# A planned instruction order, searched anew: the chain of chunks gets a margin in its due times

## The chip, the cores and the metric

One Trainium2 chip, one of its cores. The time is the device time of one execution in microseconds (us); the number for a kernel is the median of several executions. TensorE (PE) does the matrix products, PEld is its loading of weights, VectorE (DVE), ScalarE (ACT) and GpSimd (POOL) work on elements, and SyncE (SP) issues most of the transfers from and to the chip's memory.

## What is computed

Two stages, one after the other. The first is a delta rule over a sequence: 32 independent heads (4 x 8), 768 steps, head width 48. The second is a feed-forward block on the 3,072 tokens that come out.

```python
for t in range(S):                      # 768 steps, for all B*H = 32 heads
    y[t] = q[t] @ state                 # state: 48 x 48 per head
    v_old = k_n[t] @ state              # k_n: keys, normalised
    state += beta[t] * outer(k_n[t], v[t] - v_old)
x = y.reshape(3072, 384)
h = x @ w_in                            # 384 x 2048
out = (h - tanh(h)) @ w_out             # 2048 x 384
```

## The kernel before, in words

The 768 steps are cut into 24 **chunks** of 32 steps. Inside a chunk the recurrence is solved as a triangular system, and from chunk to chunk only the state is carried. For each chunk `s` TensorE runs small stages of 32 matmuls on 32- or 48-wide pieces:

- `score(s)` (line 456): products of keys with keys and queries. Four chunks make a group `g`, and `solve(g)` inverts their triangular systems on DVE, about a hundred short dependent steps (lines 501 to 588, mostly 577 and 579) that end in the transposition `tt` (line 588).
- `chain()` runs the chunks in order: keys on the state (L672), queries on the state (L689), the solution applied (L704, needs `tt` of its group and the values after the subtraction on L679), the update of the state (L719, then two additions on L745), the rest of the result (L729), and in `output()` the transposition of the chunk's result (L764) into `xt`, the tokens of the second stage.

Four chunks make a **window** of 512 tokens. For each window the feed-forward block runs 16 times two **units** on TensorE: `hidden` (L875, 9 matmuls of 128x128 on 512 columns into `ph`) and `out_units` (L925, 9 more, summed up in `po`). Between them `gate` works on ACT and DVE: tanh (L892), the subtraction (L894, which frees `ph`), and a split of the result into two parts (L900, L902). The first `F0` pairs of window 0 run as two halves of 256 columns, so that they can begin before all four chunks are there. The weights are decoded at the start (`decode`, `piece`; L823, L832, L833). Where the planner sees nothing else for TensorE early on, `warm()` puts in a **filler**, one matmul of zeros on 512 columns (L356).

All instructions are emitted by a planner, the class `Plan`. Each piece of work is an `Op` with an engine, a cost in us, its dependencies and a due time. `Plan.run` takes the engine that can begin first; among its Ops that could begin within `SLACK[engine]` of the first one it chooses the smallest `value`: the start plus `URGENCY` times the due time, plus a random part (`WHIM`), plus `STICK` on TensorE where the kind of work changes. The chosen order is fixed for each engine: at run time an engine works in this order and waits at an instruction whose inputs are missing. The planner also keeps a model of TensorE's supply with instructions (`settle`, `fetched`, `span`): 512 at the start, then 256 at a time.

Due times come from a few numbers. `start(w)` is when window `w` should begin (`SECOND + PITCH*(w-1)`), `need(s)` when chunk `s` should be ready, `unit_due(w, f)` spreads the units over a window, and `QUIRK` shifts single generators by their name. `LATCH` holds a score back until an earlier chunk is solved. `loads()` issues transfers on SP as buffers come free: keys `kc` after a score, keys `kd` after L689, values `v` after L719. `refill()` issues the last weight loads on ACT (`AHEAD`, `BEHIND`).

The due times of the chunks are these two lines (306 to 309 hold them):

```python
start = lambda w: SECOND + PITCH * (w - 1) if w else OPEN
need = lambda s: start(s // W) - SPREAD * (W - 1 - s % W) if s >= W else FIRST_NEED + NEXT_NEED * s
```

Of the kernel before, what the change touches and what calls it, by code (L numbers as in the profile page):

```python
# [26 lines left out]
W = 4  # L27
# [58 lines left out]
class Plan:  # L86
    ENGINES = ("PE", "DVE", "ACT", "POOL", "SP")
    OVERLAP = {"PE": 0.0, "DVE": 0.085, "ACT": 0.085, "POOL": 0.0, "SP": 0.0}
    VISIBLE = {"PE": 0.13, "DVE": 0.06, "ACT": 0.06, "POOL": 0.06, "SP": 0.0}
    SLACK = {"PE": 0.264, "DVE": 14.746, "ACT": 0.22, "POOL": 0.2, "SP": 0.0}  # L90

    def __init__(self, tc, nc):
        self.tc, self.nc, self.dice = tc, nc, random.Random(SEED)
# [165 lines left out]
def kernel(ctx: ExitStack, tc: tile.TileContext, kq, vk, beta, w_in, w_out, const, out):  # L259
# [46 lines left out]

    ISSUE = 0.45
    start = lambda w: SECOND + PITCH * (w - 1) if w else OPEN
    need = lambda s: start(s // W) - SPREAD * (W - 1 - s % W) if s >= W else FIRST_NEED + NEXT_NEED * s
    solve_due = lambda g: need(4 * g) - 9.0 if g else 30.0  # L310

    def opening():
# [750 lines left out]
```

## Time and profile before

| | |
|---|---|
| median of 3 executions | 622.18 us (621.96 to 623.24) |
| the profiled execution, its own time | 623.54 us |
| its span, first to last instruction | 621.8 us |
| TensorE busy | 602.0 us, 97% of the span |
| VectorE, ScalarE, GpSimd busy | 378.5, 221.5, 46.3 us |
| mean granted TensorE clock | 0.988 of full speed |
| moved from and to memory | 51.54 MB, 83 GB/s on the mean |

The profile comes from one execution. Its page gives busy times, the wait chain that ended last and the costliest groups; the trace behind it can be asked for single instructions. A row of the timeline reads: start, duration, engine, line, operation, output<-inputs, shapes, count, and in brackets the idle time before it and what ended that. A float32 stage of 32 matmuls stands in the timeline as x64, since each goes through TensorE twice.

### The profile page before, as it was taken

How to read it: one execution, taken by the hardware profiler on the slowest of the kernel's cores; microseconds unless marked ns; L12 is line 12 of the kernel's file. 1: busy time of each engine (PE TensorE's matmuls, PEld its weight loads, DVE VectorE, ACT ScalarE, POOL GpSimd, SP SyncE). 2: the span in 40 equal slices, each digit the busy share in tenths (PEclk: the TensorE clock that was granted, in tenths of full speed). 3: DMA queues.
4: the chain of work that ended last, by engine and by line, in shares of the span. 5: the costliest groups of instructions: out<-in, count | busy, mean ns of one | idle time of the engine just before them, and what ended most of it. 6: DMA issues, size and time to landing. Idle time of an engine off the chain costs nothing.

```text
span 621.8 us, 24085 instructions
## 1 busy us (share of the span) xinstructions
PE 602.0 (97%) x11120; PEld 470.8 (76%) x11120; DVE 378.5 (61%) x827; ACT 221.5 (36%) x396; POOL 46.3 (7%) x60
## 2 busy tenths in 40 slices
PE   6999999989998999999989999999999999999996
PEld 4545778867786878788778888878788887878884
DVE  2998778863789458776254788237789323432332
ACT  1324645665322342323322232333234213332332
POOL 1211100001200021000011000001100000000000
PEclk9899999999999999999999999999999999999999
DMA  9991222253332131222330212021120100010001
GB/s 321 391 374 35 99 67 74 86 163 103 97 105 70 61 113 54 63 72 76 91 108 29 77 55 78 35 64 34 55 79 35 36 2 3 3 52 1 0 1 51
DMA packets 24500, 51.54 MB, mean 83 GB/s; under 512 B 2512, under 2 KB 2640, under 8 KB 24400
## 3 DMA queue, kind: packets, MB, share of 16 engines
q1 hardware_dynamic: 22912, 46.77, 22.6%
q10 hardware_dynamic: 1488, 3.24, 1.7%
q8 instruction: 87, 1.43, 0.9%
q14 instruction: 13, 0.11, 0.1%
HBM read 45.29 MB, written 4.72 MB: 80 GB/s over the span
## 4 chain that ended last, share of the span: by engine, by line
PE 94%; DVE 2%; issue 2%; ACT 1%; DMA 0%; ACTq 0%; DVEq 0%
PE ph L875 33%; PE po L925 32%; PE po L356 7%; PE psa L456 4%; PE psa L719 3%; PE psa L704 3%; PE psy L729 3%; PE psa L672 3%; PE psy L689 2%; PE ph L832 2%; PE psa L764 1%; DVE a L579 1%; DVE tmp L577 1%; PE ph L833 0%; DMA out<-o 0%
## 5 line engine op out<-in xcount | busy, mean ns | idle before, releaser
L875 PE MATMUL ph<-xt,w 128*128 128x512 f32 (+1 forms) x900 | 217.1, 390 | 5.3 <-issue 2.7
L925 PE MATMUL po<-gh,w 128*128 128x512 f32 (+1 forms) x900 | 218.2, 390 | 1.5 <-issue 1.2
L875 PEld LDWEIGHTS ph<-xt,w 128*128 128x128 f32 x900 | 163.3, 190 | 40.6 <-issue 2.9
L925 PEld LDWEIGHTS po<-gh,w 128*128 128x128 f32 x900 | 162.1, 189 | 36.5 <-issue 1.7
L894 DVE TENSOR_TENSOR t<-ph,t 128x512 f32<-128x512 f32 (+1 forms) x100 | 66.6, 668 | 95.7 <-ACT t L892 95.5
L892 ACT ACTIVATE t<-ph 128x512 f32<-128x512 f32 (+1 forms) x100 | 58.0, 580 | 185.8 <-PE ph L875 184.8
L902 DVE TENSOR_TENSOR gh<-t,gh 128x512 fp32r<-128x512 f32 (+1 forms) x100 | 67.8, 678 | 45.3 <-ACT gh L900 44.8
L900 ACT CAST gh<-t 128x512 fp32r<-128x512 f32 (+1 forms) x100 | 60.4, 604 | 70.7 <-DVE t L894 53.1
L579 DVE TENSOR_TENSOR a<-a,tmp 128x30 f32<-128x30 f32 (+9 forms) x180 | 61.0, 339 | 4.7
L577 DVE TENSOR_TENSOR tmp<-a 128x30 f32<-128x30 f32 (+9 forms) x180 | 60.3, 335 | 4.8
L356 PE MATMUL po<-wz 128*128 128x512 bf16 x176 | 44.8, 407 | 1.1 <-DVE idle L315 1.1
L745 DVE TENSOR_TENSOR st<-st,psa 112x384 f32<-112x384 f32 x44 | 22.6, 551 | 36.2 <-PE psa L719 35.7
L356 PEld LDWEIGHTS <-wz 128*128 128x128 bf16 x176 | 17.2, 103 | 23.6 <-issue 6.2
L478 POOL TENSOR_TENSOR pq<-pq,cs 128x256 f32<-128x256 f32 x24 | 19.0, 790 | 200.0 <-ACT pq L472 200.0
L650 POOL TENSOR_TENSOR v<-v,nt 128x384 f32<-128x384 f32 x20 | 18.2, 918 | 138.2 <-DMA v<-in_vk 69.7
L456 PEld LDWEIGHTS psa<-kc 48*32 48x32 f32 x1344 | 20.4, 110 | 7.1 <-issue 6.5
L719 PEld LDWEIGHTS psa<-u_sb,v 32*48 32x48 f32 x1472 | 18.8, 120 | 9.2 <-issue 7.9
L456 PE MATMUL psa<-kc 48*32 48x64 f32 x1344 | 23.9, 222 | 0.0
L754 ACT COPY y_sb<-psy 128x384 f32<-128x384 f32 x24 | 11.5, 479 | 34.3 <-PE psy L729 34.3
L770 DVE TENSOR_TENSOR xt<-psa,xt 128x384 fp32r<-128x384 f32 x24 | 13.3, 555 | 16.1 <-ACT xt L768 16.1
L704 PEld LDWEIGHTS psa<-v,tt 32*32 32x32 f32 x1536 | 17.9, 105 | 6.3 <-issue 2.8
L719 PE MATMUL psa<-u_sb,v 32*48 32x48 f32 x1472 | 21.7, 205 | 1.0 <-issue 1.0
(61 smaller groups left out, 415.2 us busy)
## 6 DMA issues: line engine op xcount, KB each, us to landing
kd<-in_kq SPq DMA_DIRECT2D x23, 512.0 KB, 4.0
kc<-in_kq SPq DMA_DIRECT2D x21, 512.0 KB, 3.8
v<-in_vk SPq DMA_DIRECT2D x24, 384.0 KB, 3.5
raw<-in_w_in SPq DMA_DIRECT2D x6, 768.0 KB, 11.8
raw<-in_w_out SPq DMA_DIRECT2D x6, 768.0 KB, 12.1
out<-o SPq DMA_DIRECT2D x18, 256.0 KB, 2.0
raw<-in_w_in ACTq DMA_DIRECT2D x2, 768.0 KB, 4.5
raw<-in_w_out ACTq DMA_DIRECT2D x2, 768.0 KB, 4.5
```

The costliest lines, as they stand in the source:

```text
L356: nc.tensor.matmul((ps if own else pos[w][0][0]).rearrange("p (a b) -> p a b", a=4), wz, wide, start=own, stop=own, skip_group_check=not own)
L456: nc.tensor.matmul(ps[quad[b], h, :], k[:, 0], k, start=True, stop=True)
L577: nc.vector.tensor_tensor(tv, col.broadcast_to(shape), row.broadcast_to(shape), ALU.mult)
L579: nc.vector.tensor_tensor(below, below, tv, ALU.add)
L704: nc.tensor.matmul(pu[rows, h, :], tt[rows, 8 * r + h, :], v[rows, h, :], start=True, stop=True)
L719: nc.tensor.matmul(hv(sums[b // 2][0])[HALF[b % 2], h, :], kt[rows, h, :], u_sb[rows, h, :], start=True, stop=True)
L875: nc.tensor.matmul(p, wi[f][:, a, ct, :], xt[:, b, ct, part], start=(ct == 0 and i == 0), stop=(ct == NC - 1 and i == 2))
L892: nc.scalar.activation(t_, p, AF.Tanh)
L894: nc.vector.tensor_tensor(t_, p, t_, ALU.subtract)
L900: nc.scalar.copy(gh[:, 0, :n], t_)
L902: nc.vector.tensor_tensor(gh[:, 1, :n], t_, gh[:, 0, :n].bitcast(F32), ALU.subtract)
L925: nc.tensor.matmul(po[c][:, part], wo[f][:, a, 128 * c:128 * c + 128], gh[:, b, :n], start=(f == 0 and i == 0 and z < 1), stop=(ended.get( ...
```

## The change

The program is the same; only the planner's numbers and one due time differ. `need(s)` loses a new constant `MARGIN` (7.6 us) for the chunks of window 1 and later. At the same time `SECOND`, `PITCH`, `SPREAD`, `LEAD`, `SLACK`, `STICK`, `HOLD`, `GUARD`, `FIRST_NEED`, `NEXT_NEED`, `EAGER`, `LATCH` and many `QUIRK` entries change, the random part goes (`WHIM` 0.5 to 0.0), `F0` rises from 4 to 6, the first loads stand in another order, and two weight loads move from SP to ACT (`AHEAD` 12 to 10).

```diff
-    SLACK = {"PE": 0.264, "DVE": 14.746, "ACT": 0.22, "POOL": 0.2, "SP": 0.0}
+    SLACK = {"PE": 0.211, "DVE": 14.4, "ACT": 0.344, "POOL": 0.2, "SP": 0.0}
...
-    need = lambda s: start(s // W) - SPREAD * (W - 1 - s % W) if s >= W else FIRST_NEED + NEXT_NEED * s
+    need = lambda s: start(s // W) - MARGIN - SPREAD * (W - 1 - s % W) if s >= W else FIRST_NEED + NEXT_NEED * s
...
-BURN, LATCH = 0, ((8, 0), (8, 5), (13, 5))
+BURN, LATCH = 0, ((9, 4), (10, 2), (16, 2))
...
-OPEN, SECOND, EARLY, PITCH, SPREAD, URGENCY, FETCH, QUEUED, FILL, LEAD, STICK = 60.5, 164.6, 4.4, 83.3, 19.1, 0.049, 3.5, 3.3, 150.0, 37.4, 0.1
-WARM, HOLD, GUARD, F0 = 120.0, 150.0, 0.28, 4
+OPEN, SECOND, EARLY, PITCH, SPREAD, URGENCY, FETCH, QUEUED, FILL, LEAD, STICK = 61.2, 176.5, 5.4, 87.8, 15.5, 0.049, 3.5, 3.3, 150.0, 29.7, 0.2
+WARM, HOLD, GUARD, F0 = 120.0, 90.0, 0.3, 6
...
-WHIM, SEED = 0.5, 240318
-FIRST_NEED, NEXT_NEED, EAGER, JOIN = 69.6, -6.7, 88.6, -61.2
-LOW, SPARE = True, 8
-AHEAD, BEHIND = 12, 3
+WHIM, SEED = 0.0, 495840
+FIRST_NEED, NEXT_NEED, EAGER, JOIN = 67.7, -1.8, -27.1, -62.0
+LOW, SPARE, MARGIN = True, 8, 7.6
+AHEAD, BEHIND = 10, 4
```

What the planner makes of it moves on every engine. Three places follow; in them the numbers behind names are buffers, `kd5` and `kc8` belong to chunks 5 and 8, `tt2` to group 2.

TensorE at chunk 5, before: the rows from the keys on the state to the next scores.

```order
L672 MATMUL psa1_88<-st_83,kd5_1224 32x48 x32
L689 MATMUL psy_2227<-st_83,kd5_1224 32x48 x32
L704 MATMUL psa0_87<-v_1126,tt1_1896 32x48 x32
L875 MATMUL ph_2303<-xt0_1030,w8_1804 128x512 x9
L875 MATMUL ph_2315<-xt0_1030,w10_2003 128x512 x9
L456 MATMUL psa1_88<-kc8_486 32x64 x32
L925 MATMUL po0_1300<-gh_2330,w9_1895 128x512 x3
L925 MATMUL po1_1301<-gh_2330,w9_1895 128x512 x3
L925 MATMUL po2_1302<-gh_2330,w9_1895 128x512 x3
L456 MATMUL psa0_87<-kc9_533 32x64 x32
```

The same place with the change:

```order
L672 MATMUL psa1_88<-st_83,kd5_1344 32x48 x32
L689 MATMUL psy_2274<-st_83,kd5_1344 32x48 x32
L925 MATMUL po0_1225<-gh_2236,w9_2079 128x512 x3
L925 MATMUL po1_1226<-gh_2236,w9_2079 128x512 x3
L925 MATMUL po2_1227<-gh_2236,w9_2079 128x512 x3
L875 MATMUL ph_2326<-xt0_942,w10_1881 128x512 x9
L704 MATMUL psa0_87<-v_1114,tt1_2041 32x48 x32
L456 MATMUL psa1_88<-kc8_493 32x64 x32
L875 MATMUL ph_2416<-xt0_942,w10_1881 128x512 x9
```

Before, three small stages (L672, L689, L704) stood in a row and two units behind them; now two units stand between the second and the third stage.

TensorE at the end of the program, window 5, before:

```order
L875 MATMUL ph_8830<-xt5_7737,w14_2263 128x512 x9
L925 MATMUL po0_8528<-gh_8828,w13_2139 128x512 x3
L925 MATMUL po1_8529<-gh_8828,w13_2139 128x512 x3
L925 MATMUL po2_8530<-gh_8828,w13_2139 128x512 x3
L875 MATMUL ph_8855<-xt5_7737,w14_2263 128x512 x9
L925 MATMUL po0_8528<-gh_8853,w15_2369 128x512 x3
L925 MATMUL po1_8529<-gh_8853,w15_2369 128x512 x3
L925 MATMUL po2_8530<-gh_8853,w15_2369 128x512 x3
L925 MATMUL po0_8528<-gh_8878,w15_2369 128x512 x3
L925 MATMUL po1_8529<-gh_8878,w15_2369 128x512 x3
L925 MATMUL po2_8530<-gh_8878,w15_2369 128x512 x3
```

And with the change:

```order
L875 MATMUL ph_8855<-xt5_7808,w12_2145 128x512 x9
L875 MATMUL ph_8865<-xt5_7808,w14_2341 128x512 x9
L875 MATMUL ph_8880<-xt5_7808,w14_2341 128x512 x9
L925 MATMUL po0_8582<-gh_8878,w13_2234 128x512 x3
L925 MATMUL po1_8583<-gh_8878,w13_2234 128x512 x3
L925 MATMUL po2_8584<-gh_8878,w13_2234 128x512 x3
L925 MATMUL po0_8582<-gh_8894,w15_2434 128x512 x3
L925 MATMUL po1_8583<-gh_8894,w15_2434 128x512 x3
L925 MATMUL po2_8584<-gh_8894,w15_2434 128x512 x3
L925 MATMUL po0_8582<-gh_8918,w15_2434 128x512 x3
L925 MATMUL po1_8583<-gh_8918,w15_2434 128x512 x3
L925 MATMUL po2_8584<-gh_8918,w15_2434 128x512 x3
```

Units of L875 and L925 took turns, and the last two L925 units followed the last L875 unit; now three of each stand together, and three L925 units follow the last L875 unit.

VectorE where the solution of group 2 (`tt2`) is finished, before:

```order
L577 TENSOR_TENSOR tmp_3355<-a2_2548 128x30
L579 TENSOR_TENSOR a2_2548<-a2_2548,tmp_3355 128x30
L894 TENSOR_TENSOR t_3317<-ph_3285,t_3317 128x512
L582 TENSOR_TENSOR a2_2548<-a2_2548,gm_2554 128x1024
L902 TENSOR_TENSOR gh_3360<-t_3317,gh_3360 128x512
L588 STREAM_TRANSPOSE tt2_3375<-a2_2548 128x32x32
L894 TENSOR_TENSOR t_3372<-ph_3345,t_3372 128x512
L894 TENSOR_TENSOR t_3386<-ph_3362,t_3386 128x512
L902 TENSOR_TENSOR gh_3390<-t_3372,gh_3390 128x512
L902 TENSOR_TENSOR gh_3424<-t_3386,gh_3424 128x512
```

With the change:

```order
L894 TENSOR_TENSOR t_3374<-ph_3343,t_3374 128x512
L577 TENSOR_TENSOR tmp_3475<-a2_2818 128x30
L579 TENSOR_TENSOR a2_2818<-a2_2818,tmp_3475 128x30
L582 TENSOR_TENSOR a2_2818<-a2_2818,gm_2824 128x1024
L902 TENSOR_TENSOR gh_3478<-t_3374,gh_3478 128x512
L679 TENSOR_TENSOR v_2217<-v_2217,psa0_87 128x384
L588 STREAM_TRANSPOSE tt2_3510<-a2_2818 128x32x32
L894 TENSOR_TENSOR t_3392<-ph_3364,t_3392 128x512
L894 TENSOR_TENSOR t_3508<-ph_3482,t_3508 128x512
L902 TENSOR_TENSOR gh_3578<-t_3392,gh_3578 128x512
```

The subtraction for chunk 8 (L679) now stands just ahead of `tt2`, and two subtractions of the gate (L894) still stand behind it.

Over the whole program, the counts that differ are these: fillers 176 before and 166 now; matmuls of L875 and of L925 on 512 columns 828 each before and 810 now, on 256 columns 72 each before and 108 now (and the gate's work on ACT and DVE with them). When the result of the fourth chunk of windows 1 to 5 is transposed (L764), TensorE has run 32, 64, 96, 127 and 160 units before the change, and 32, 63, 96, 128 and 159 with it (two halves counted as one unit).

More of the change, by code (lines that the diff above doesn't have):

```diff
@@ L996 @@
     return plan
-QUIRK = {'hidden0.1.2': 33, 'add7': 12, 'score5': -17, 'score6': -29, 'decode8': 35, 'vsub6': 18, 'out_units0.1.3': 40, 'piece13': -25, 'prep0': 3, 'mask3': -34, 'output3': -1, 'join0': 33, 'output4': -18, 'hidden0.-1.0': 12, 'output0': 14, 'chain7': 12, 'out_units0.0.1': 25, 'vsub3': -38, 'join6': 0, 'decode7': 14, 'prep6': 25, 'decode9': -40, 'piece8': 2, 'hidden0.-1.2': 10, 'vsub0': -18, 'hidden0.-1.3': 10, 'add0': 15, 'piece15': 40, 'prep7': -15, 'solve0': 8, 'decode14': -30, 'solve1': 5, 'gate0.-1.1': 2, 'mask1': -3, 'mask7': -22, 'join1': -2, 'mask6': 0, 'join2': -5, 'decode4': -26, 'out_units0.-1.0': 30, 'piece4': 2, 'out_units0.0.2': 22, 'score1': 3, 'hidden0.1.3': -15, 'decode6': 3, 'gate0.1.3': 7, 'chain0': -4, 'join3': 7, 'vsub1': 25, 'decode1': 24, 'out_units0.-1.3': 30, 'piece6': -10, 'gate0.-1.0': -22, 'hidden0.-1.1': 0, 'output7': 35, 'out_units0.-1.1': -5, 'gate0.1.2': -6, 'gate0.1.1': 2, 'decode2': -8, 'decode15': -3, 'vsub5': 20, 'score2': -5, 'score7': -34, 'decode11': 0, 'mask2': 0, 'score4': 0, 'piece11': 10, 'hidden0.0.3': -3, 'piece9': 10, 'triangle0': -10, 'decode5': 20, 'gate0.1.0': -25, 'piece1': -5, 'decode10': 40, 'chain2': 3, 'gate0.0.2': 18, 'join7': -20, 'vsub7': 4, 'chain5': -6, 'output5': 2, 'vsub4': 5, 'out_units0.1.1': 2, 'piece14': 32, 'gate0.0.3': -10, 'add5': -15, 'add2': -7, 'join5': -22, 'out_units0.0.0': -10, 'score0': 0, 'out_units0.1.0': -20, 'output6': -20, 'decode12': 0, 'gate0.-1.2': 2, 'hidden0.0.2': 10, 'hidden0.1.0': -2, 'decode0': 25, 'output2': -10, 'piece0': 20, 'piece2': -2, 'mask4': 2, 'add4': -20, 'out_units0.0.3': -5, 'mask0': 8, 'add3': -2, 'piece10': -5, 'join4': 5, 'out_units0.-1.2': -2, 'hidden0.1.1': 2, 'prep2': -10}
@@ L1000 @@
-BURN, LATCH = 0, ((8, 0), (8, 5), (13, 5))
+QUIRK = {'hidden0.1.2': 31, 'add7': 12, 'score5': -17, 'score6': -29, 'decode8': 35, 'vsub6': 38, 'piece13': -5, 'prep0': 3, 'output3': -1, 'join0': 43, 'output4': -18, 'output0': 14, 'chain7': 12, 'out_units0.0.1': 25, 'vsub3': -38, 'decode7': 14, 'prep6': 25, 'decode9': -50, 'piece8': 2, 'hidden0.-1.2': 30, 'vsub0': -13, 'hidden0.-1.3': 10, 'add0': 15, 'piece15': 40, 'prep7': -15, 'solve0': 8, 'decode14': -30, 'solve1': 5, 'gate0.-1.1': -3, 'mask1': -3, 'mask7': -22, 'join1': 8, 'mask6': 0, 'join2': -5, 'decode4': -26, 'out_units0.-1.0': 30, 'piece4': -3, 'out_units0.0.2': 32, 'score1': 8, 'hidden0.1.3': -20, 'decode6': 3, 'gate0.1.3': 7, 'chain0': -4, 'join3': 7, 'vsub1': 25, 'decode1': 34, 'out_units0.-1.3': 30, 'piece6': -10, 'hidden0.-1.1': 2, 'output7': 35, 'out_units0.-1.1': -7, 'gate0.1.2': -6, 'gate0.1.1': 2, 'decode2': -8, 'decode15': -3, 'vsub5': 18, 'score2': -5, 'score7': -34, 'decode11': -20, 'mask2': 0, 'score4': 0, 'piece11': 10, 'hidden0.0.3': -3, 'piece9': 12, 'triangle0': -10, 'decode5': 40, 'gate0.1.0': -25, 'piece1': -5, 'decode10': 40, 'chain2': 3, 'gate0.0.2': 18, 'join7': -20, 'chain5': -6, 'output5': 2, 'vsub4': 7, 'out_units0.1.1': 7, 'piece14': 32, 'gate0.0.3': -10, 'add5': -15, 'add2': -7, 'join5': -22, 'out_units0.0.0': -10, 'out_units0.1.0': -15, 'output6': -20, 'decode12': 0, 'gate0.-1.2': 2, 'hidden0.0.2': 10, 'hidden0.1.0': -2, 'decode0': 25, 'output2': -10, 'piece0': 40, 'piece2': -2, 'mask4': 2, 'add4': -20, 'out_units0.0.3': -5, 'mask0': 8, 'add3': -2, 'piece10': -5, 'join4': 5, 'out_units0.-1.2': -2, 'hidden0.1.1': 2, 'prep2': -10, 'hidden0.0.0': -20, 'output1': -20, 'answer1': -20, 'chain4': -5, 'vsub2': -20, 'prep4': -8, 'out_units0.1.3': 20, 'gate0.0.0': 2, 'chain1': 20, 'mask5': 10, 'answer4': -40, 'mask3': 20, 'answer0': 2, 'score0': 5, 'chain6': -2, 'gate0.-1.0': 5}
@@ L1001 @@
+BURN, LATCH = 0, ((9, 4), (10, 2), (16, 2))
 HALVED = ()
 SOLS, PQS, UYS, CB, LB, GHS, KCS, KDS, VS = 4, 13, 4, 3, 1, 2, 3, 3, 4
-OPEN, SECOND, EARLY, PITCH, SPREAD, URGENCY, FETCH, QUEUED, FILL, LEAD, STICK = 60.5, 164.6, 4.4, 83.3, 19.1, 0.049, 3.5, 3.3, 150.0, 37.4, 0.1
-WARM, HOLD, GUARD, F0 = 120.0, 150.0, 0.28, 4
-FIRST = ['k0', 'k1', 'k2', 'k3', 'b0', 'v1', 'v3', 'k4', 'w2', 'w4', 'k6', 'w0', 'w3', 'k7', 'v0', 'k5', 'w1', 'v2', 'b1']
-WHIM, SEED = 0.5, 240318
-FIRST_NEED, NEXT_NEED, EAGER, JOIN = 69.6, -6.7, 88.6, -61.2
@@ L1008 @@
-LOW, SPARE = True, 8
-AHEAD, BEHIND = 12, 3
+OPEN, SECOND, EARLY, PITCH, SPREAD, URGENCY, FETCH, QUEUED, FILL, LEAD, STICK = 61.2, 176.5, 5.4, 87.8, 15.5, 0.049, 3.5, 3.3, 150.0, 29.7, 0.2
+WARM, HOLD, GUARD, F0 = 120.0, 90.0, 0.3, 6
+FIRST = ['k0', 'k1', 'k2', 'k3', 'b0', 'k4', 'v1', 'w4', 'v3', 'w2', 'k7', 'w0', 'k6', 'w3', 'v0', 'b1', 'v2', 'k5', 'w1']
+WHIM, SEED = 0.0, 495840
+FIRST_NEED, NEXT_NEED, EAGER, JOIN = 67.7, -1.8, -27.1, -62.0
+LOW, SPARE, MARGIN = True, 8, 7.6
+AHEAD, BEHIND = 10, 4
```

## The prediction

> **What bounds the kernel now.** I read the page first, then TensorE's waits, then its timeline.
>
> ```profile
> span 621.8 us, 24085 instructions
> ...
> PE 602.0 (97%) x11120; PEld 470.8 (76%) x11120; DVE 378.5 (61%) x827; ACT 221.5 (36%) x396; POOL 46.3 (7%) x60
> ...
> PEclk9899999999999999999999999999999999999999
> ...
> q8 instruction: 87, 1.43, 0.9%
> ```
>
> TensorE is busy for 97% of the span and no other engine comes near. So the time is what TensorE has to run, plus what it waits, plus what it loses at a lower clock. Its waits by cause:
>
> ```profile
> PE psa L456 <- issue: 3.4, 1, 3.4
> PE ph L875 <- issue: 2.7, 1, 2.7
> PE psy L689 <- issue: 2.1, 2, 1.6
> PE ph L875 <- DVE t L894: 1.9, 1, 1.9
> PE po L925 <- issue: 1.2, 1, 1.2
> ...
> PE psa L719 <- issue: 1.0, 1, 1.0
> ```
>
> Work of another engine ends only one long wait, the 1.9 us. Most are "issue": TensorE waited for nothing that the profile shows. They come after runs of small stages:
>
> ```profile
> 132.60 0.88 PE L672 MATMUL psa<-st,kd 48*32 48x48 f32 x64
> ...
> 135.03 0.96 PE L875 MATMUL ph<-xt,w 128*128 128x512 f32 x3
> 138.69 5.20 PE L875 MATMUL ph<-xt,w 128*128 128x512 f32 x15 [2.70 <-issue]
> 143.82 0.37 PE L456 MATMUL psa<-kc 48*32 48x64 f32 x12
> ```
>
> ```profile
> 319.63 0.86 PE L672 MATMUL psa<-st,kd 48*32 48x48 f32 x64
> 320.31 0.76 PE L689 MATMUL psy<-st,kd 48*32 48x48 f32 x53
> 322.65 0.36 PE L689 MATMUL psy<-st,kd 48*32 48x48 f32 x11 [1.57 <-issue]
> 322.94 3.63 PE L925 MATMUL po<-gh,w 128*128 128x512 f32 x9
> 326.37 2.54 PE L875 MATMUL ph<-xt,w 128*128 128x512 f32 x9
> ```
>
> I read them as waits for instructions. The q8 row moved 87 blocks of 1.43 MB / 87 = 16.4 KB, and TensorE has 2 x 11,120 = 22,240 instructions, 256 for each block. I counted them along the planned order (a stage 64 matmuls and 64 loads, so 128; a unit 18; a transposition 6; semaphore instructions too): all six "issue" waits, the 3.4 us included, stand 192 to 194 past a multiple of 256. TensorE crosses from block to block there. From one crossing to the end of the wait at the next went 138.69 - 133.3 = 5.3 us in the first case and 322.65 - 319.5 = 3.2 us in the second. So I estimate 3.2 us for a block, and up to 5.3 beside data loads. A block holds two stages (1.7 us) when it is all stages, and one unit more makes it about 4. Before, exactly three blocks are short: 2.7 us of work (chunk 5), 1.6 (chunk 13) and 2.4 (chunk 17), and each ended in a wait, 2.7, 1.57 and 1.2 us.
>
> The clock pays again:
>
> ```profile
> 134.00:145.00 11.00, 8.25 (x163) 6.31 (x152) 4.69 (x7) 4.58 (x8) 0.00 (x0) 0.84 0.32 119
> 145.00:186.00 41.00, 41.00 (x1081) 32.65 (x1081) 28.89 (x72) 15.11 (x30) 7.86 (x10) 1.00 0.37 111
> ...
> 320.00:330.00 10.00, 8.43 (x196) 6.66 (x184) 5.17 (x14) 1.50 (x4) 1.99 (x2) 0.83 0.37 110
> ```
>
> The column before the last two is the granted clock: 1.00 in a stretch without waits, 0.84 and 0.83 around the two longest late ones. The Trainium skill ("TensorE: Matmul & The Clock Gate", Part 1) lets the clock fall only after an idle window of about 3.4 us. By it a wait of 1.57 us costs only itself and the clock's share of my sum is 0, but the 0.83 above speaks against that here.
>
> **The change, part by part.** All sums go against the profiled execution, 623.54 us for a span of 621.8; the median of the runs shown, 622.18, is 1.4 lower.
>
> *1. What TensorE has to run.*
>
> ```profile
> 33.06 20.89 PE L356 MATMUL po<-wz 128*128 128x512 bf16 x96
> ...
> 100.32 3.46 PE L925 MATMUL po<-gh,w 128*128 128x256 f32 x27
> 103.62 5.35 PE L875 MATMUL ph<-xt,w 128*128 128x256 f32 x27
> ```
>
> ```profile
> 347.01 2.33 PE L925 MATMUL po<-gh,w 128*128 128x512 f32 x9
> 349.27 0.93 PE L719 MATMUL psa<-u_sb,v 32*48 32x48 f32 x64
> ...
> 605.51 2.20 PE L875 MATMUL ph<-xt,w 128*128 128x512 f32 x9
> 607.55 2.20 PE L925 MATMUL po<-gh,w 128*128 128x512 f32 x9
> ```
>
> Ten fillers fewer at 20.89 / 96 = 0.218 us: -2.2. (The 140 up to the first L704 stay, so the chain begins at the same time.) A half unit takes (103.62 - 100.32) / 3 = 1.10 us, a unit 2.04 from start to start: two pairs of units become halves, 4 x (2.20 - 2.04) = +0.6. A unit alone between stages takes 349.27 - 347.01 = 2.26, so each run of units costs 0.22 at its edges; the order has 82 runs before and 75 now: -1.5. Stages, pairs of the weight decoding and transpositions keep their number. Sum **-3.0** (-3.1, and I keep the lower figure).
>
> *2. Short blocks.* The waits behind runs of stages and the block waits at L719 (1.0) and at the other L689 (2.1 - 1.6 = 0.5) add up to 7.0 us. The lower clock is seen as 143.82 - 135.03 = 8.8 us for two units, that is 1.8 over 2.7 + 4.3, and as 326.37 - 322.94 = 3.4 for one, 1.2 over 2.26: 3.0. Together 10.0. Counted in the same way, the new order has no block under 2.9 us of work; three lie at 2.9 to 3.3 (chunks 2, 17 and 22). It still has two triples of stages at chunks 6 and 13, but only one crossing falls in each. For the three I take 0.5 each (1.5), for meetings with data loads as much as before (1.0 + 0.5 = 1.5), and 0.5 for the clock: 3.5 stay. The ends are 0 and all 10.0. Sum **-6.5**.
>
> *3. Waits for other engines.*
>
> ```profile
> 193.91 0.68 DVE L894 TENSOR_TENSOR t<-ph,t 128x512 f32<-128x512 f32 x1
> ...
> 194.65 2.35 PE L875 MATMUL ph<-xt,w 128*128 128x512 f32 x9 [1.95 <-DVE t L894]
> ```
>
> ```profile
> 155.82 1.25 DVE L501 STREAM_TRANSPOSE a<-gs 128x1024 f32<-128x1024 f32 x1 [0.40 <-ACT gs L468]
> ...
> 204.13 2.09 DVE L588 STREAM_TRANSPOSE tt<-a 128x1024 f32<-128x1024 f32 x1
> 207.13 0.88 PE L704 MATMUL psa<-v,tt 32*32 32x48 f32 x64
> ```
>
> The third of three L875 in a row waited, since L894 stood in DVE's queue behind steps of `solve(2)`. In the new order three L925 stand behind such a run (6.1 us, in which DVE can work off the steps ahead of the next L894). The wait of 1.9 goes. But of 21 fillers that covered steps of the chain at chunks 0 to 4 only 7 are left; decoding and halves stand there instead, and these need ACT and DVE themselves; I take 1.0 for new waits, between 0 and, as an upper end, 5.0 from `solve(2)` (below). Sum **-0.9**.
>
> *4. The end.*
>
> ```profile
> 611.63 2.78 PE L925 MATMUL po<-gh,w 128*128 128x512 f32 x10
> 614.64 2.11 PE L925 MATMUL po<-gh,w 128*128 128x512 f32 x8 [0.23 <-DVE gh L902]
> ```
>
> Two units in 614.64 + 2.11 - 611.63 = 5.1 us, where 4.1 is their work: the last one waited for its gate, with one L925 as cover. Now two stand ahead of it. Sum **-1.0**. With three L875 in a row the third needs the first one's `ph`, free within 2.04 us (a tanh and a subtraction, 0.60 and 0.69 us): I cost that at nothing; if DVE is late it is item 3 again.
>
> The moved loads (SP's order at the start, two weight loads on ACT's queue) precede work that TensorE covers with 140 fillers; I cost them at nothing, and what they could cost is a block that meets one, in item 2.
>
> Sum: -3.0 - 6.5 - 0.9 - 1.0 = -11.4: 612.1 on the profiled execution, 610.8 on the median. I say **611**.
>
> **The rivals.**
>
> *The "issue" waits return.* If they don't hang on the density of stages, item 2 is 0 and the time is 622.2 - 3.0 - 0.9 - 1.0 = 617.3. The Trainium skill ("Runtime: NRT & Kernel Launch", Instruction fetch mechanics) gives TensorE room for 2,048 instructions and calls the crossing of a block mostly hidden, which would lead here. Against it: the wait of 3.4 us is already at instruction 448, and the three shortest blocks are the three that waited. 0.15.
>
> *`solve(2)` comes late.* It went from 155.82 to 206.22, 50.4 us, and L704 of chunk 8 needs it at 207.13. From the last score of group 2 to that L704 the new order puts about 46 us on TensorE (17 units, 11 stages and their edges). DVE was busy for 44 us there:
>
> ```profile
> 156.40:207.10 50.70, 48.22 (x1054) 38.66 (x1052) 44.41 (x112) 14.89 (x28) 5.46 (x7) 1.00 0.27 83
> ```
>
> Between the two transpositions of this group it now has some 3 us less of other work, so it can just be done. If it takes 50.4 again, the wait is 4 to 5 us: 615 to 616. 0.12.
>
> *More blocks meet loads (slower).* Both orders have some 32 blocks with 3.6 to 4.3 us of work, less than the 5.3 that a block took beside a load. Loads follow the stages that free their buffers (L689, L456, L719), so where the new phases put a load onto a crossing they do so again and again. It decides at 11.4 / 32 = 0.36 us more for each; at the 0.5 us or so of the shortest wait, and 0.2 of clock, the sum is +22, so 633. Before, only two of such blocks waited. 0.04.
>
> *The change doesn't do what it says.* `MARGIN` is 7.6 us, but `SECOND` and `PITCH` put window 1 at 11.9 and window 5 at 29.9 us later. The chain then stands where it stood against the units (32, 63, 96, 128, 159 of them against 32, 64, 96, 127, 160). So no gain can come from an earlier chain; if new waits of 11 us then take the place of the old ones, the time is within 0.2%: 622. 0.04.
>
> **How the numbers follow.** My case 0.65 (606 to 614), the waits that return 0.15, `solve(2)` 0.12, slower 0.04, no effect 0.04. The likeliest gives 611. The low end takes off all that stays in items 2 and 3 (3.5 + 1.0): 606.5. The high end covers both rivals of 615 to 617: 617.5. Beyond 0.2% (1.2 us), about what a measurement of this kernel can tell from no change: faster 0.92, same 0.04, slower 0.04.
>
> **What the profile after would show.** Item 1: 166 fillers, and a unit alone still 2.26. Item 2: "issue" waits after the first 20 us under 3 us in sum, none over 1.5, and a granted clock near 1.00 from 100 us on. Item 3: no wait for L894 over 1 us, and no wait at L704 of chunk 8. Item 4: the last two units in 4.1 us. I would be wrong if issue waits come at blocks with a unit in them, or if TensorE waits for DVE in runs of three L875.

## The result, and the profile after

The changed kernel takes **617.24 us** (median of 4, 616.37 to 617.75) and the kernel before, run beside it, 622.07 (621.78 to 623.24): a ratio of 0.9915, 95% interval 0.9893 to 0.9937. The forecast was 611.0, with a range of 606.5 to 617.5. The change is faster, but by 4.8 us (0.9%) and not by 11.

The page of the changed kernel, profiled execution of 617.75 us:

```profile
span 615.7 us, 24171 instructions
...
PE 598.0 (97%) x11146; PEld 471.6 (77%) x11146; DVE 382.4 (62%) x831; ACT 221.5 (36%) x400; POOL 43.6 (7%) x60
...
PEclk8999899999999999999999999999999999999999
...
L356 PE MATMUL po<-wz 128*128 128x512 bf16 x166 | 40.9, 399 | 1.1 <-DVE idle L315 1.1
```

TensorE is still the bound, with 166 fillers. Its waits after the first 20 us, as line, cause, total, times and longest:

```profile
PE psa L672 <- issue: 2.8, 2, 2.0
PE ph L875 <- DVE t L894: 1.0, 1, 1.0
PE psy L729 <- issue: 1.0, 1, 1.0
PE psy L689 <- issue: 0.9, 2, 0.5
PE ph L875 <- ACT xt L768: 0.6, 1, 0.6
...
PE ph L875 <- issue: 0.2, 1, 0.2
```

The issue waits add up to 4.9 us, where under 3 had been forecast, and the longest is 2.0, where none over 1.5 had been. The timeline of TensorE shows where they are. The longest first, at chunk 2:

```profile
69.76 0.45 PE L672 MATMUL psa<-st,kd 48*32 48x48 f32 x21
72.25 0.70 PE L672 MATMUL psa<-st,kd 48*32 48x48 f32 x43 [2.04 <-issue]
72.87 4.98 PE L875 MATMUL ph<-xt,w 128*128 128x256 f32 x27
```

And the last ones, at chunks 16 to 18:

```profile
400.73 0.28 PE L729 MATMUL psy<-u_sb,pq 32*32 32x48 f32 x6 [0.95 <-issue]
400.94 2.35 PE L875 MATMUL ph<-xt,w 128*128 128x512 f32 x9
...
405.36 0.44 PE L689 MATMUL psy<-st,kd 48*32 48x48 f32 x19 [0.43 <-issue]
...
424.54 0.28 PE L672 MATMUL psa<-st,kd 48*32 48x48 f32 x6 [0.72 <-issue]
```

The block from 400.7 to 405.4 holds a whole unit (L875) beside its stages, and TensorE waited at its end all the same. That is one of the two things of which the prediction said that they would make it wrong.

The windows view of the stretch behind the longest wait (before the last two columns stands the granted clock):

```profile
69.70:78.00 8.30, 6.26 (x95) 6.01 (x95) 3.68 (x9) 4.74 (x9) 0.83 (x1) 0.79 0.11 37
...
100.00:190.00 90.00, 88.31 (x1946) 73.39 (x1945) 67.70 (x141) 45.29 (x80) 8.69 (x11) 1.00 0.31 103
```

From 100 us on the clock is 1.00, as forecast; in the 8.3 us at chunk 2 it is 0.79 on the mean (the last section looks closer).

To compare the two traces I took, for every group of TensorE instructions, the time from its start to the start of the next one, and as its content the median of the same between like neighbours in the kernel before. What is over that is its loss (losses of 0.2 us and more are listed here). The row on content therefore repeats the forecast's way of counting; what tests it is that only 0.1 us of the span is left over at the end of the table. In the two profiled executions:

| term | forecast | before | after | found |
|---|---|---|---|---|
| 1. content | -3.0 | 548.6 | 545.6 | -3.0 |
| 2. issue waits and the clock behind them | -6.5 | 11.3 | 8.0 | -3.3 |
| 3. waits for other engines | -0.9 | 3.4 | 5.3 | +1.9 |
| 4. the end | -1.0 | 1.0 | 0 | -1.0 |
| first L704 of chunk 0 | 0 | 53.89 | 53.26 | -0.6 |
| losses under 0.2 | 0 | | | -0.1 |
| span | -11.4 | 621.8 | 615.7 | -6.1 |

The 0.6 at the start is not the change's: over the twelve profiled executions of this document other than those of the two kernels on the margin, the first L704 starts between 52.9 and 54.1, also among kernels with the same order up to there.

### The profile page after: what moved, and what is told of

The parts are those of the page before. It is cut to its first block, busy times and chain, and to the rows that moved or that the text cites. A ratio compares the mean times of both kernels' runs of the same rounds, so it can differ in the third digit from the quotient of the medians.

```text
span 615.7 us, 24171 instructions
## 1 busy us (share of the span) xinstructions
PE 598.0 (97%) x11146; PEld 471.6 (77%) x11146; DVE 382.4 (62%) x831; ACT 221.5 (36%) x400; POOL 43.6 (7%) x60
## 4 chain that ended last, share of the span: by engine, by line
PE 94%; DMA 2%; DVE 1%; issue 1%; ACT 1%; SPq 0%; ACTq 0%
PE po L925 33%; PE ph L875 33%; PE po L356 6%; PE psa L456 4%; PE psa L719 3%; PE psy L729 3%; PE psa L672 3%; PE psa L704 3%; PE psy L689 3%; PE ph L832 2%; PE psa L764 1%; DMA kd<-in_kq 1%; DVE a L579 0%; PE ph L833 0%; DVE tmp L577 0%
## 5 line engine op out<-in xcount | busy, mean ns | idle before, releaser
L875 PE MATMUL ph<-xt,w 128*128 128x512 f32 (+1 forms) x918 | 215.7, 385 | 2.2 <-DVE t L894 1.0
L925 PE MATMUL po<-gh,w 128*128 128x512 f32 (+1 forms) x918 | 213.8, 383 | 0.0
L875 PEld LDWEIGHTS ph<-xt,w 128*128 128x128 f32 x918 | 164.3, 190 | 36.8 <-DVE t L894 1.4
L925 PEld LDWEIGHTS po<-gh,w 128*128 128x128 f32 x918 | 162.8, 188 | 33.6 <-DVE gh L902 1.1
L894 DVE TENSOR_TENSOR t<-ph,t 128x512 f32<-128x512 f32 (+1 forms) x102 | 66.7, 656 | 91.4 <-ACT t L892 91.0
L356 PE MATMUL po<-wz 128*128 128x512 bf16 x166 | 40.9, 399 | 1.1 <-DVE idle L315 1.1
L719 PEld LDWEIGHTS psa<-u_sb,v 32*48 32x48 f32 x1472 | 18.6, 119 | 8.8 <-issue 7.2
L672 PE MATMUL psa<-st,kd 48*32 48x48 f32 x1472 | 20.8, 204 | 2.8 <-issue 2.8
L672 PEld LDWEIGHTS psa<-st,kd 48*32 48x32 f32 x1472 | 17.5, 107 | 7.6 <-issue 6.7
```

Source lines behind the costliest of these rows:

```text
L356: nc.tensor.matmul((ps if own else pos[w][0][0]).rearrange("p (a b) -> p a b", a=4), wz, wide, start=own, stop=own, skip_group_check=not own)
L672: nc.tensor.matmul(pk[quad[b], h, :], kd[rows, 0, 2 * h + pr, :], st[rows, pr, h, :], start=True, stop=True)
L719: nc.tensor.matmul(hv(sums[b // 2][0])[HALF[b % 2], h, :], kt[rows, h, :], u_sb[rows, h, :], start=True, stop=True)
L875: nc.tensor.matmul(p, wi[f][:, a, ct, :], xt[:, b, ct, part], start=(ct == 0 and i == 0), stop=(ct == NC - 1 and i == 2))
L894: nc.vector.tensor_tensor(t_, p, t_, ALU.subtract)
L925: nc.tensor.matmul(po[c][:, part], wo[f][:, a, 128 * c:128 * c + 128], gh[:, b, :n], start=(f == 0 and i == 0 and z < 1), stop=(ended.get( ...
```

## The experiments

In these kernels (but the two on the margin) the planner's picks are written out as a list that it follows, so that a single pick can be moved and all else stays. The diffs of moved picks show TensorE's order. Two theories stand against each other on the issue waits: **A**, a block of 256 instructions makes TensorE wait when the work in it is too short, whatever else happens (the prediction's item 2); and **C**, its fetch also comes late behind data loads in flight, so that blocks with a unit in them wait too. **B** is that density has nothing to do with it. A block is *dispatched* when TensorE crosses into the block ahead of it; the trace doesn't show that moment, so it is placed by the count of instructions. All ratios are to the kernel before, run on the same chip in the same job.

### Moving units into the short blocks of the kernel before

b_moved, at chunk 5 (at chunks 13 and 17 an L925 goes from behind L689 to ahead of it):

```diff
 L672  chunk 5
 L689  chunk 5
+L875
 L704  chunk 5
 L875
-L875
 L456
```

> The kernel before with its own order written out and three units moved by one place: one L875 from behind L704 to ahead of it at chunk 5, one L925 from behind L689 to ahead of it at chunk 13, and one at chunk 17. Each of the three short blocks of instructions then has 3.8 to 3.9 us of work instead of 2.4, 1.7 and 2.4. Theory A (a block with less work than its fetch takes makes TensorE wait, and the waits pull the clock down): the losses of 4.5 us at 135, 3.4 at 320 to 329 and 1.5 at 413 go, and three more edges of runs cost 0.7: 8.7 us less, 613.4. Rival B (the waits come from something else, such as data loads that fall there in any case): they stay at the same crossings, and the time is 622 to 623.

Measured: 617.28 us (616.04 to 618.95), ratio 0.9926 (0.9903 to 0.9949). The timeline at chunk 13 and at chunk 5:

```profile
317.12 2.37 PE L925 MATMUL po<-gh,w 128*128 128x512 f32 x9
319.41 0.88 PE L689 MATMUL psy<-st,kd 48*32 48x48 f32 x64
```

```profile
131.94 0.86 PE L689 MATMUL psy<-st,kd 48*32 48x48 f32 x64
132.74 2.37 PE L875 MATMUL ph<-xt,w 128*128 128x512 f32 x9
135.03 0.86 PE L704 MATMUL psa<-v,tt 32*32 32x48 f32 x58
137.09 0.28 PE L704 MATMUL psa<-v,tt 32*32 32x48 f32 x6 [1.20 <-issue]
```

At chunks 13 and 17 the waits and the slow units behind them are gone (3.4 and 1.5 us), so B falls. At chunk 5, 4.5 became 1.5: there one unit more was not enough. The same trace shows what was on the way: a load of weights (768 KB, on queue q10), issued by ACT, and behind it a load of keys, issued by SP at 132.87. First ACT's row, then the queues from 131.9 to 134.8 us:

```profile
131.18 0.37 ACTq L391 DMA_DIRECT2D raw<-in_w_out  x1
```

```profile
q10 hardware_dynamic: 248, 0.74, 82.2%
q1 hardware_dynamic: 7, 0.01, 1.3%
```

The block was dispatched at about 131.9, and its 16 KB packet (queue q8 in the DMA view, read in stretches of 0.2 us) moved only at 134.9, 3.0 us later, when nearly all of the weights (0.74 MB) and almost nothing of the keys (0.01 MB) had moved; most packets of this trace moved 0.6 to 1.5 us after the dispatch. From the packet to the end of the wait went 2.2 us. A alone has no room for this.

The medians give a gain of 4.8 where 8.7 was expected, the two profiled executions 7.5 (spans of 621.8 and 614.3): the one of the kernel before lies 1.4 us above its median, and that of b_moved 1.2 below. The rest at chunk 5 is 1.5 of what is missing. Not every wait hangs on the order alone: that of 0.96 at L719 of chunk 3 in the kernel before is not there in b_moved, although no pick is moved ahead of it, while that at L689 of chunk 8 is in both (0.53 and 0.58).

### The moved weight load, put back and put in

a_early puts it back in the changed kernel; b_late puts it into the kernel before:

```diff
 a_early
-                load_pair(n)
+                [load_pair(m) for m in ((9, 10, 11) if n == 9 else (n,))]
...
-            load_pair(i, "ACT")
+            i > 11 and load_pair(i, "ACT")
```

```diff
 b_late
-                load_pair(n)
+                n > 9 or load_pair(n)
...
-            nc.scalar.activation(lo, lw, AF.Copy, scale=7.49 / 255.0)
+            nc.scalar.activation(lo, lw, AF.Copy, scale=7.49 / 255.0); i in (5, 6) and load_pair(i + 5, "ACT")
```

> The changed kernel in its own order, but the weight loads raw10 and raw11 are issued by SP right behind raw9, as in the kernel before, and no longer by ACT at 65.5 us and later. Theory C (the fetch of a block comes late behind a data load in flight; the moved load of 768 KB is what made the wait at L672 of chunk 2): the wait of 2.04 us there goes and with it the clock's share of the 1.37 in the L875 behind it: 617.2 - 3.4 = 613.8. Rival A alone (only the work in a block counts): the block has the same 4.5 us of work, the wait stays, 617.2. Rival D (the loads cost something at the start instead, where SP issues two more of them ahead of the loads for chunk 8): up to 617.2 again, with the first L704 of chunk 0 later than 53.3 us.

> The kernel before in its own order, but raw10 is loaded by ACT right behind the L810 that starts at 65.57 us, and raw11 behind the next L810, instead of by SP at the start: the one move of loads that the change made, put into the kernel before. The block that is dispatched at 66.75 (in L719 of chunk 1) and used at L672 of chunk 2, 70.5, has 3.8 us of work. Theory C (a block's fetch comes late behind a data load in flight): the packet of 16 KB moves nearly whole behind the 768 KB, a wait of about 2 us appears at L672 of chunk 2 and the units behind it run at the lower clock, together 3 to 3.5 us: 625.1 to 625.6. Rival A (only the work in a block counts): no wait, 622.1.

Measured: a_early 613.01 us (612.14 to 613.56), ratio 0.9853 (0.9828 to 0.9878), which is 4.2 under the changed kernel; b_late 624.59 us (621.45 to 626.83, 12 runs), ratio 1.0036 (1.0017 to 1.0054), about 2 over the kernel before, where 3 to 3.5 had been expected: a wait came, but the clock stayed at 1.00 behind it. TensorE at chunk 2 in a_early:

```profile
69.70 0.88 PE L672 MATMUL psa<-st,kd 48*32 48x48 f32 x64
70.52 3.62 PE L875 MATMUL ph<-xt,w 128*128 128x256 f32 x27
```

And in b_late, where the kernel before has no wait:

```profile
71.10 0.44 PE L672 MATMUL psa<-st,kd 48*32 48x48 f32 x19
72.99 0.66 PE L672 MATMUL psa<-st,kd 48*32 48x48 f32 x43 [1.45 <-issue]
```

The same load makes a wait at the same stage in either kernel (2.04 and 1.45 us), and taking it away takes the wait away: C holds, A alone falls. The packet itself is seen in the DMA view. In the changed kernel ACT issues raw10 at 65.54 (`q10`) and SP a load of v at 66.90; the block is dispatched at about 66.2. The queues' rows for 66.2 to 69.7 us, then for 69.7 to 70.1:

```profile
q10 hardware_dynamic: 395, 0.78, 73.8%
q1 hardware_dynamic: 190, 0.15, 13.9%
```

```profile
q1 hardware_dynamic: 50, 0.15, 94.5%
q8 instruction: 1, 0.02, 15.9%
```

For 3.5 us the weights move and no instruction packet does; it comes with the last of them, and 2.3 us later L672 goes on. In a_early the packet of this block moves 1.0 us after its dispatch.

### Without the late loads

a_noload is the changed kernel without them (kc and kd from chunk 14 on, v from chunk 16 on; the stages read older tiles), a_both has the edit of a_early too:

```diff
-        kc = ld.tile([128, 2, 16, C], F32, tag=tag, ...
-        nc.sync.dma_start(kc, kq[s]...
+        kc = table[13][0] if s > 13 else ld.tile([128, 2, 16, C], F32, tag=tag, ...
+        s > 13 or nc.sync.dma_start(kc, kq[s]...
...
-        nc.sync.dma_start(both, vk[s])
+        s > 15 or nc.sync.dma_start(both, vk[s])
```

> The changed kernel in its own order, but the loads of kc and kd from chunk 14 on and of v from chunk 16 on are left out: the stages read the keys of chunk 13 and the v of four chunks before, so that the output of these chunks is not the reference's, and the work of every engine is otherwise the same. From chunk 14 on the losses at issue waits are 0.31, 0.72, 1.21, 0.68, 0.33 and 0.97, 4.2 us. Theory C (fetches late behind data loads): all of them go but for that of the block with 3.1 us of work at 420 (0.3) and perhaps that at 366, where an output of 256 KB is in flight (0.7): 3.2 to 3.9 less, 613.3 to 614.0. Rival A alone (only the work in a block counts): they stay, 617.2. The waits before 340 us are the same in both.

> a_early and a_noload together: the changed kernel in its own order with raw10 and raw11 loaded by SP at the start, and without the loads of kc and kd from chunk 14 on and of v from chunk 16 on (those stages read older tiles, so the output of these chunks is not the reference's). If data loads in flight are what kept my estimate of the issue waits too low (3.5 us with the clock, where 7.7 were found), the two savings add up: 617.2 - 4.2 - 3.0 = 610.0, which is about what I had forecast for the change. If they are the same time saved twice, or other waits move in: 612 to 613.

Measured: a_noload 614.19 us (612.84 to 614.68), ratio 0.9871 (0.9845 to 0.9897); a_both 611.18 us (610.87 to 612.11), ratio 0.9820 (0.9801 to 0.9839). From 340 to 430 us the changed kernel has issue waits of 1.0 (L729), 0.9 (L689), 0.7 (L672) and 0.2 (L875), 2.8 in all. The list of TensorE's waits in the same stretch of a_noload has one line:

```profile
PE po L925 <- issue: 0.3, 1, 0.3
```

With TensorE's order unchanged, 2.8 us of waits shrink to 0.3. The two savings together make 6.1 us; 4.2 + 3.1 would be 7.3, and in a_both one block, at L672 of chunk 18, still waits 0.8. It waited 0.7 with the loads and 0.3 in a_noload (there at the L925 that follows), so this block is short by itself. From 413 to 418.3 us of a_both, up to the end of that wait, one packet of instructions is all that moves on any queue:

```profile
q8 instruction: 1, 0.02, 1.1%
```

With both groups of loads out of the way the new order takes 611.2, within 0.2 of what I had forecast for it. That agreement is in part chance: issue waits after the first 20 us are 1.2 us there, where 3.5 with the clock were to stay, and the waits for L894 and xt, which the forecast had priced too low, are all still there (1.0, 0.6 and 0.3).

### The loads moved in time, and the units spread

Both start from a_early. a_vlate keeps all loads and changes only their order on SP; a_dense changes none of them, moves ten units and one L704, for instance at chunk 16, and takes over the moved L894 of a_dve (next part):

```diff
 a_vlate, SP's queue, each time
-v   chunk s+4   (free after L719 of chunk s)
 kd  chunk s+4   (free after L689 of chunk s+1)
+v   chunk s+4
```

```diff
 a_dense, chunks 15 and 16
-L925
 L719  chunk 15
 L729  chunk 15
 L925
 L764  chunk 15
 L672  chunk 16
+L925
 L689  chunk 16
```

> The kernel of a_early (613.0), with TensorE's order unchanged, in which each load of v stands on SP's queue behind the load of kd that followed it: it then starts when L689 of the next chunk is done, and no longer when L719 is. No load is left out. In the profiled execution of a_early four of the five late blocks from chunk 14 on (losses 0.58, 0.99, 0.40, 0.86) had a load of v issued within 0.6 us of their dispatch. Theory C (late behind loads): these go, and the loads of v then meet long runs of units: 613.0 - 2.8 = 610.2, down to 609.5 if the 0.8 at L689 of chunk 3 goes too. Rival G (a later load of v only meets another block): 612 to 614.

> a_early with the L894 of a_dve, and with ten units and one L704 moved by a few places, so that the blocks of instructions that waited in a_early (at chunks 3, 15, 16, 17 and 18) have one unit more: 6 us of work instead of 4, and none of these under 4.0. No load is moved. By the durations, eight more edges of runs cost 1.7 us. Theory A and C together (a block waits when its work is less than the delay of its packet and some 2.2 us): the losses of 0.81, 0.58, 0.99, 0.40, 0.43 and 0.86 go, and 1.3 at the L894: 613.0 - 4.1 - 1.3 + 1.7 = 609.3. Rival B (the waits hang on the loads alone and stay where they are): 613.0 + 1.7 - 1.3 = 613.4.

Measured: a_vlate 616.19 us (613.24 to 619.24), ratio 0.9888 (0.9863 to 0.9913); a_dense 615.06 us (614.74 to 615.21), ratio 0.9879 (0.9861 to 0.9897). Neither gains on a_early: their medians lie 3.2 and 2.1 us above its 613.01, though the intervals of the ratios overlap, and both miss all that had been expected of them. In a_vlate the waits at chunks 15 and 16 shrink from 0.32 and 0.78 to nothing and 0.35, but each load that stood behind the moved ones is late too. SP, then TensorE:

```profile
154.39 1.79 SPq L372 DMA_DIRECT2D v<-in_vk  x1
156.27 8.19 SPq L364 DMA_DIRECT2D kc<-in_kq  x3
```

```profile
163.12 0.92 PE L456 MATMUL psa<-kc 48*32 48x64 f32 x46 [1.53 <-issue]
163.98 3.82 PE L875 MATMUL ph<-xt,w 128*128 128x512 f32 x9
```

Three loads of kc follow each other, a block there waits 1.53, and the unit behind it runs 1.5 us too long; the wait at L689 of chunk 3 grows from 0.55 in a_early to 1.58. That is the mechanism of rival G, at a higher price than its 612 to 614. In a_dense the list of waits after 20 us is:

```profile
PE po L925 <- ACT gh L900: 1.6, 2, 1.1
PE po L925 <- DVE gh L902: 0.9, 3, 0.4
PE ph L875 <- ACT xt L768: 0.6, 1, 0.6
PE ph L832 <- ACT w L836: 0.6, 1, 0.6
```

Not one issue wait is left. So a unit more per block made these blocks safe from their loads, as A and C together say. But the price was forecast too low: beside 1.7 us for the edges of shorter runs, the L925 that were pulled ahead now stand close behind their own L875 and wait for the gate (losses of 1.3, 0.5 and 0.6 at chunk 17), and smaller waits came at chunks 3, 8 and 16. The span grew from 611.3 to 613.0.

### The waits at the switch of windows

In the changed kernel the first three L875 of the second window lost 0.8 and 1.7 us. a_dve moves one subtraction on DVE; a_cover moves two picks of TensorE; a_best is a_cover with a_vlate:

```diff
 a_dve, DVE
+L894  first unit of the window
 L577, L579  (two pairs, solve of group 2)
-L894  first unit of the window
```

```diff
 a_cover, TensorE
-L925  last of window 0
 L729  chunk 7
 L672  chunk 8
 L764  chunk 7
+L925  last of window 0
 L875
 L875
+L689  chunk 8
 L875
-L689  chunk 8
```

> The changed kernel with one thing moved: the tanh and the subtraction L894 behind the first unit of the second window stand four steps of the solve earlier on DVE (TensorE's order is unchanged). In the profiled execution this L894 began at 188.11 although its tanh was done at 186.45, and the third L875 of the run waited 1.0 us for it, 1.66 us lost in all. Theory H (the order of DVE's queue makes that wait): the wait and 1.3 to 1.6 us go, 615.7; the wait for xt of 0.57 stays. Rival F (DVE has more work there than time, and L704 of chunk 8 or a later L875 then waits as long): 617.2.

> The changed kernel with two picks moved at the switch to the second window of units, and nothing else: the last L925 of the first window goes from ahead of L729 of chunk 7 to behind its transposition, and L689 of chunk 8 from behind the three L875 to between the second and the third. Theory E (there the run of three L875 has too little ahead of it: the first waits for xt, the third for L894 in DVE's queue, 0.82 + 1.66 us in the profiled execution): both go, one more edge costs 0.2: 617.2 - 2.3 = 614.9. Rival F (DVE with its solve steps is what bounds there, and the wait comes back at a later L875 or L704): 617.2.

> a_vlate and a_cover together. If the terms add up: 610.2 - 2.3 = 607.9. If TensorE then waits at the switch for DVE in another place, or the loads of v meet other blocks: 610 to 612.

Measured: a_dve 617.97 us (614.09 to 619.06), ratio 0.9918 (0.9894 to 0.9942); a_cover 616.30 us (615.92 to 616.77), 0.9894 (0.9882 to 0.9907); a_best 613.84 us (613.14 to 614.21), 0.9857 (0.9842 to 0.9871). The switch in the changed kernel on TensorE, and on DVE:

```profile
183.11 4.75 PE L875 MATMUL ph<-xt,w 128*128 128x512 f32 x18 [0.57 <-ACT xt L768]
188.85 1.43 PE L875 MATMUL ph<-xt,w 128*128 128x512 f32 x5 [1.00 <-DVE t L894]
```

```profile
187.81 0.39 DVE L579 TENSOR_TENSOR a<-a,tmp 128x220 f32<-128x220 f32 x1
188.11 0.68 DVE L894 TENSOR_TENSOR t<-ph,t 128x512 f32<-128x512 f32 x1
```

and TensorE in a_dve:

```profile
183.51 6.79 PE L875 MATMUL ph<-xt,w 128*128 128x512 f32 x27 [0.57 <-ACT xt L768]
...
195.34 2.12 PE L925 MATMUL po<-gh,w 128*128 128x512 f32 x8 [0.25 <-DVE gh L902]
```

The wait for L894 goes when L894 no longer stands behind the steps of the solve, so the order of DVE's queue makes it (H). But 1.0 us of the 1.3 comes back in the L925 behind it, which wait for their gate. In a_cover the losses at the switch and up to chunk 9 went from 2.7 to 3.2. Rival F fits both better: DVE, which works on `solve(2)`, is the bound there, and a cover in one place opens another. From 183 to 207 us it is busy for 22.5 of 24 us in the changed kernel and in a_cover alike. The 0.9 us by which the median of a_cover is lower is not clear of the spread (the intervals of the two ratios overlap). a_best was to reach 607.9 if the terms added up, or 610 to 612 if not; it takes about as long as a_early, so the two together bring no gain that could be seen.

### The margin by itself

```diff
 b_margin (before)
-need = lambda s: start(s // W) - SPREAD * ...
+need = lambda s: start(s // W) - MARGIN - SPREAD * ...
...
+MARGIN = 7.6
 a_margin0 (after)
-LOW, SPARE, MARGIN = True, 8, 7.6
+LOW, SPARE, MARGIN = True, 8, 0.0
```

> The kernel before with the margin of 7.6 us in the due times of the chain and nothing else of the change: the planner orders everything anew with its old numbers. By the durations of the kernel before, the new order has 6.7 us more for TensorE to run (more fillers and shorter runs of units), and ten blocks of instructions have under 3.6 us of work instead of five, three of them 1.8 to 2.8. If a step of the change is worth what its words say (chain ahead of its units), the time is at or under 622. If the order as a whole decides (content and blocks), it is 622 + 6.7 + about 3 = 630 to 634, and the margin by itself gains nothing.

> The changed kernel with the margin set to 0 and every other number of the change kept: the planner orders everything anew. By the durations the new order has 8.6 us more for TensorE to run, and three blocks of instructions have 2.0 to 2.1 us of work, which cost about 1.2 us each and as much again by the clock. If the margin is what makes the gain, or if the order as a whole does: in both cases 617.2 + 8.6 + about 5 = 628 to 632. If the margin does nothing: 617.

Measured: b_margin 629.46 us (628.22 to 630.85), ratio 1.0120 (1.0092 to 1.0148); a_margin0 642.28 us (640.40 to 644.09), 1.0307 (1.0277 to 1.0336). The margin alone makes the kernel before slower, and the changed kernel without it is slower than both. Either way the planner's other numbers no longer fit: 214 and 208 fillers instead of 176 and 166. These are one new order each, and no other number of the planner was changed by itself, so what the margin is worth as such is not shown; the gain belongs to the order as a whole. For a_margin0 I was 10 us too low: the sum had the content and the short blocks, but not the waits for xt and for gates, which came back at nearly every switch of windows and in the last run of units, and too little for the clock: it is granted at 0.50 for 20.5 us after the start (10.2 of them on end, from 183.9), which loses up to 10 us against full speed.

## Why the prediction was off

**What held.** Item 1: 166 fillers, a content 3.0 us smaller, and a unit between stages at 2.26 to 2.29. Item 4: the last three L925 run without a wait, and 1.0 is gone. `solve(2)` was in time: no wait at L704 of chunk 8. The three short blocks of the kernel before did cost what they were said to cost, and are gone (b_moved shows the cause at chunks 13 and 17; the block of chunk 5 met a load of weights as well).

**Item 2 failed, in two of its prices.** The step read: "for meetings with data loads as much as before (1.0 + 0.5 = 1.5)". Found: 8.0 us where 3.5 were to stay, and most of it in meetings: of the 4.9 us of waits, the 2.0 at chunk 2 go without the weight load (a_early), and of the 2.8 behind 340 us 2.0 to 2.5 go without the late loads (a_both, a_noload). What is left of these is the block that ends at L672 of chunk 18, which is short by itself. I had the mechanism in hand, "3.2 us for a block, and up to 5.3 beside data loads", and set it against the wrong question. I counted blocks that are short even without a load (under 3.2), though by the prediction's own count some 32 blocks lie between 3.6 and 4.3, where a meeting decides; and I took their number of meetings from one execution of another order. How often they meet hangs on where the loads' issues fall, and that changes with the order. The second price was "I cost them at nothing", of the moved weight loads; a block that meets one was named there, but no term of the sum was given to it. Put back, the load saves 4.2 us (a_early), put into the kernel before it costs about 2 (b_late). I had priced it as work of SP and ACT, covered by 140 fillers, and not as traffic at the place to which it moved: it left the start, where nothing waits, for 65.5 us, between chunks 1 and 2.

**Item 3 failed by sign.** "The wait of 1.9 goes", because three L925 behind a run give DVE time. They do, but for the second run; the first run of the window has nothing behind it yet, and 2.5 us are lost there in place of 2.2. "With three L875 in a row the third needs the first one's `ph` ... I cost that at nothing" left out the queue: L894 came 2.3 us after its tanh had begun, behind solve steps. That was the second thing said to make the prediction wrong. Another 1.6 us are small losses at chunk 3, where decoding and halves stand in the place of fillers; 1.0 had been put there.

**The rivals.** The first one gave 617.3 if item 2 were nothing, and the time is 617.24, but that is not what happened: item 2 brought 3.3, and 2.8 of item 3 were missing. It hit the number by luck. Its reason, that the waits don't hang on density, is refuted by b_moved and a_dense. The page named for it, "Runtime: NRT & Kernel Launch" of the Trainium skill (Instruction fetch mechanics), calls the crossing of a block mostly hidden; here it was, in all but some seven of 87 blocks (after the first 20 us), and those cost 8 us. The slower rival had the right mechanism, blocks that meet loads, and needed 0.36 us for each of 32 blocks; it was seven of them at 0.3 to 3.8. "The change doesn't do what it says" fits what the margin did by itself (b_margin), and was wrong on the time. The other page of the Trainium skill, "TensorE: Matmul & The Clock Gate" (Part 1), lets the clock fall only after an idle window of about 3.4 us. Here a wait of 2.04 us was followed by a clock of 0.79 over 8.3 us, so its rule would again have priced that part at 0.

**The better kernel.** a_early, the change without its move of two weight loads, takes 613.0 us, against 617.2 and 622.1.

## What to carry to other kernels

A transfer that is moved off a crowded start is not free: see what TensorE runs where it lands, and above all whether a block of instructions is fetched there. Here that cost 4.2 us of a forecast gain of 11. Where instructions are streamed in blocks and a kernel is made of small matmuls, compare the work in each block with the time of a fetch *behind the largest load that can be in flight*, not with the undisturbed one. Cover taken from one place is missing in another: the spreading of units that ended all issue waits cost more in edges and gates than the waits.

## What was not expected of the hardware

A block's packet of 16.4 KB usually moves 0.5 to 1.5 us after its dispatch, one block ahead, but behind loads of 384 to 768 KB up to 3.7 us after it. TensorE goes on 2.2 to 3.0 us after the packet has begun to move; that holds for every issue wait in the twelve traces named above (72.25 in the changed kernel, 137.09 in b_moved and 363.80 in a_early, for instance, after packets at 69.9, 134.9 and 361.6). It is the strongest sign that all these waits are waits for instructions.

The clock falls by whole stretches of 3.41 us. The windows view of the changed kernel around the longest wait, with the granted clock before the last two columns:

```profile
69.44:72.85 3.41, 1.37 (x66) 0.88 (x64) 0.56 (x1) 2.40 (x4) 0.00 (x1) 1.00 0.30 116
72.85:76.26 3.41, 3.41 (x22) 3.39 (x17) 2.13 (x5) 1.06 (x3) 0.83 (x1) 0.50 0.03 5
76.26:79.68 3.42, 3.42 (x30) 3.42 (x30) 2.11 (x8) 2.51 (x7) 0.00 (x0) 1.00 0.19 23
```

Half the clock for 3.41 us is 1.7 us at most; the units behind waits of 2.04, 1.77 (a_noload) and 1.53 us (a_vlate) ran 1.4 to 1.5 us too long. The kernel before has two such stretches after the first 20 us and up to its last units (from 139.32 and 323.64), the changed kernel one, a_early none. The length of the wait does not decide: behind 1.83 us in a_dve, at the same stage as the first two, behind 1.58 in a_vlate and behind 2.03 for L894 in b_moved, the clock stayed at 1.00. What fits better is how long TensorE was busy in the 3.41 us before. Counted off in steps of 3.41 us from the last change of the clock, in all traces of this document, a stretch at full clock with 0.6 to 1.8 us of matmuls was each time followed by 0.50 (1.37 above), one with 2.2 us and more never, and between these both occur (1.83 and 1.88 us in a_vlate: 1.00 and 0.50). So waits of one length, 1.77 and 1.83 us at the same stage, can differ by 1.4 us in their cost, by where they fall in these steps.

Executions of one kernel spread by up to 6 us (a_vlate 613.24 to 619.24) where its order has blocks near the limit, and by 0.5 in a_dense, which has no issue waits after the first 20 us. That small shifts decide whether a load meets a block, and that this is the cause of the spread, is argued and was not tried; a_cover, with seven such waits in its trace, spreads by only 0.9.
